# Three moves in the order of an attention and MLP kernel: a score tile, two squares and a quarter of a weight load

## The chip, the cores and the metric

The kernel runs on one core of a Trainium2 chip. The metric is the device time of one execution in microseconds; it is the median over several executions. The engines are named as in the profile: PE (matrix products), ACT (activation functions), DVE (vector work), POOL (vector work, and the software DMA queue q0), SP (issues DMAs on the hardware queue q1). Each engine does its instructions in the order of the program; only semaphores tie the engines together.

## The reference

Inputs are q, k, v of shape (8, 12, 448, 64), gains for the norms, and the weights of an MLP. The reference, cut to what matters:

```python
def rmsnorm(x, g):
    return x / sqrt(mean(x * x, -1) + 1e-06) * g
scores = matmul(rmsnorm(q, g_q), rmsnorm(k, g_k).T) / 8     # 448 x 448 for each of 96 heads
attn   = softmax(scores)
x      = matmul(attn, v)          # heads side by side: 3584 rows of 768
h      = x @ w_in                 # 768 x 2048
out    = (maximum(h, 0) + alpha * minimum(h, 0)) @ w_out    # 2048 x 768
```

## The kernel before

The work of attention is cut into 24 groups y of four heads, three groups (G = 3) for each of 8 batches. What happens to a group, with the function and the line that the profile shows:

- `load_qk` (L105): four DMAs on SP's queue bring q and k of the group as float32, each tile (`nat`) in two halves. Six `nat` tiles exist, so that three groups fit.
- `square` (L148, POOL from group 2 on), `reduce` (L154, DVE), `root` (L165 and L166, ACT: a logarithm and an exponential), `scale` (L171, POOL for most groups): the norm. Results are `sq`, `ss`, `rr`, `qs`.
- `turn_dma` (L181): from group 6 on (TD = 6) two DMA transposes on SP's queue turn `qs` into `qT` and `kT`; `turn` (L192, DVE) then multiplies `kT` by the gains. For earlier groups PE transposes (`tps`, L206) and DVE copies (L215, L217).
- `score` (L232, PE): one of seven tiles j of a group's scores, in PSUM (`sc`, two slots). `soft` (L246, ACT): its exponential, `expT`.
- `den` and `attv` (L261, PE): the sums and the products with v (`dn`, `av`, `avb`); `log` and `invert` (L278, L283, ACT); the normed result goes to `xT` (L310, L312, DVE).

The MLP is cut into units. `up(b, ft)` makes one of 16 tiles of h for batch b (six matmuls, L327, into `hT`, or `hTb`/`hTa` in other PSUM banks), then `ah` (L354, ACT) and `gT` (L355, DVE). `down(b0, t, oh)` makes 128 rows and one half oh of the outputs: 16 matmuls over the tiles of `gT` and `w_out_sb` (L365, `op` or `opa`), a copy (`osb`, L377) and DMAs of the output (L385).

A planner puts the score tiles into bursts n, and MLP units into the gap after each burst (`gaps[n]`). Its list `prep` holds calls that go ahead of a burst, its list `post` those that go behind the units of its gap. `at(n, ...)` and `after(n, ...)` fill these lists:

```python
def after(n, f, *a):
    post.setdefault(max(int(n), 0), []).append((f, a))
```

The bursts that matter here:

| burst | score tiles (group, tile) | other attention work | units in its gap |
|---|---|---|---|
| 10 (`lead`) | (3,0) (3,1) (3,2) | den and attv of group 2 | up 0 to 4 of batch 0 |
| 11 | (3,3) (3,4) | root and scale of group 5 | up 5, 6 |
| 12 | (3,5) (3,6) | PE transpose of group 4; v of batch 1 is loaded ahead of it | up 7, 8 |
| 13 | (4,0) (4,1) | reduce of group 6 | up 9, 10, 11 |
| 14 | (4,2) (4,3) | root and scale of group 6, its DMA transposes | up 12, 13 |
| 15 | (4,4) (4,5) | PE transpose of group 5 | up 14, 15 |
| 16, 17 | (4,6) (5,0) to (5,3) | den of groups 3 and 4; root of group 7 | down (0, t) for oh = 0, t = 0, 1 |
| 18 | (5,4) (5,5) (5,6) (6,0) | attv of groups 3 and 4 | down t = 2, oh = 0 |
| 19, 20 | group 6 | den, attv of group 5 | down t = 0 and t = 1, oh = 1 |
| 21 | (7,0) (7,1) | reduces of group 9 | up 0 to 3 of batch 1 |

Burst 10, in the text "group 2's burst", is special. Batch 0's attention is completed in it, so the MLP can begin. Units 0 to 3 are begun ahead of it with the products that don't need group 2 (`begin`, L342), and their remainder follows as units 0 to 3 of the gap. Units 2 and 3 share one PSUM tile, `hTb`. The third score tile (3,2) and its exponential are put between the units by the list `late`, whose entries hold the number of units after which a call is made.

w_in and w_out are loaded on POOL's queue, with a cast to float16. `load_w_out(c)` brings a quarter of w_out: c // 2 is the half oh of the outputs, c % 2 the half of the 16 weight tiles. `first` is 10, the burst of `lead`. The loads of v (`vt`, L114) use the same queue.

Of the kernel before, what the change touches and what calls it, by code (L numbers as in the profile page):

```python
# [21 lines left out]
def kernel(  # L22
# [19 lines left out]
    G = HH // 2  # L42
# [135 lines left out]
    def turn_dma(y):  # L178
        for nm in "qk":
            t = att.tile([128, J, 2, 64], FP16, name=f"{nm}T", tag=f"{nm}T", bufs=4)  # L180
            nc.sync.dma_start(  # L181
                out=t.rearrange("p j g c -> p j (g c)"),
                in_=qs[y, nm].rearrange("p j h d -> p (j h d)"),
                transpose=True,
            )
            qkT[y, nm] = t
# [38 lines left out]
    def score(y, j):  # L225
        qT, kT = qkT[y, "q"], qkT[y, "k"]
        sc = pss.tile([128, 2, 512], FP32, name="sc", tag="sc")
        m = 64 if y < EARLY else 32
        for c in range(64 // m):
            for par in range(2):  # L230
                for g in range(2):
                    nc.tensor.matmul(  # L232
                        out=sc[ds(64 * g + m * c, m), par, :S].rearrange(
                            "p (j c) -> p j c", j=J
                        ),
                        lhsT=kT[ds(64 * par, 64), j, g, ts(c, m)],
                        rhs=qT[ds(64 * par, 64), :, g, :],
                        start=True,
                        stop=True,
                    )  # L240
        scs[y, j] = sc

    def soft(y, j):
        if j == 0:
            expT[y] = att.tile([128, J, 2, S], FP16, name="expT", tag="expT", bufs=EB)
        nc.scalar.activation(  # L246
            out=expT[y][:, j], in_=scs[y, j][:, :, :S], func=AF.Exp,
            scale=QK_SCALE, bias=expb[:, 0:1],
        )
# [19 lines left out]
    def den(ys):  # L269
        dn = psa.tile([128, 2, 512], FP32, name="dn", tag="acc")  # L270
        over_keys(
            (dn[:, 0], dn[:, 1]), ys, lambda g, y, par, c, j: ones[ds(64 * g, 64), c]
        )
        rden[ys] = dn

    def log(ys):
        r = att.tile([128, 2, S], FP32, name="rden", tag="rden")
        nc.scalar.activation(out=r, in_=rden[ys][:, :, :S], func=AF.Ln)  # L278
        rden[ys] = r
# [55 lines left out]
    def begin(ft):  # L335

        if ft < 2:
            begun[ft] = bank("hT", False)
        elif ft == 2:
            t = psa.tile([128, 2, 512], FP32, name="hTb", tag="acc")  # L340
            begun[2], begun[3] = t[:, 0], t[:, 1]
        up_part(begun[ft], 0, ft, 0, G - 1)  # L342
# [66 lines left out]
    while m < NG * J or steps:  # L409
        n = len(bursts)  # L410
        while steps:
# [14 lines left out]
        late = both or n in dens and n in avs or any(  # L426
            y >= G for y in dens.get(n, avs.get(n, ()))
        )
        limit = 2 + late + (both and avs[n][0] >= G)
        bursts.append([])  # L430
        while len(bursts[n]) < limit and m < NG * J:
            y, j = divmod(m, J)
# [13 lines left out]
    def at(n, f, *a):  # L446
        prep.setdefault(max(int(n), 0), []).append((f, a))

    def after(n, f, *a):
        post.setdefault(max(int(n), 0), []).append((f, a))  # L450
# [9 lines left out]
    for y in range(G, NG):  # L460

        early = y < G + 2
        if early:
            n = turn_at[y - 1] + 1
        elif y == G + 2:
            n = den_at[G - 1]
        elif y == 2 * G:
            n = turn_at[y] - 4
        elif y % G == 1:
            n = den_at[y - 4] - 1  # L470
        elif y % G:
            n = den_at[y - G]
        else:
            n = av_at[y - 4]
        at(n - (6 if early else 4 if y <= 3 * G else 5), load_qk, y)
        for nm in "qk":
            after(n - 2, square, y, nm)
            if early:
                after(n, reduce, y, nm)
            else:  # L480
                jobs.setdefault(n, []).append((reduce, (y, nm)))
        roots[n + 1] = y
# [29 lines left out]
    first = av_at[G - 1]  # L512
# [92 lines left out]
    after(7, load_w_in, 2)  # L605
    after(8, load_w_in, 3)
    for c in range(4):
        after(first + c // 2 * 2, load_w_out, c)
    roots[3] = 2

    since = 2
    for n in range(NB):
        for f, a in prep.get(n, ()):
            f(*a)
        tiles = bursts[n]

        lead = n == den_at[G - 1]
        first_tiles = tiles[: 2 if lead else split.get(n, 2)]
        for t in first_tiles:
            score(*t)  # L620
            if n == den_at[G - 1] - 1 and t == tiles[-1]:
                begin(0)
                begin(1)
            elif lead and t == tiles[0]:
                soft(*t)
                den(dens[n])
                attv(avs[n], 0, True, (log, invert))
            elif lead and t == tiles[1]:
                begin(2)
        plain = lead or n not in dens and n not in avs  # L630
        wait = plain and not lead and gaps[n] and gaps[n][0][0] is up
        if lead:
            begin(3)
        for t in tiles[:1] if wait else tiles[1:2] if lead else first_tiles:
            soft(*t)
        if n in dens and not lead:
            den(dens[n])
        if n in avs and not lead:

            for half in (1, 0) if avs[n] == (0, 1) else (0,):  # L640
                attv(avs[n], half)
        for t in () if lead else tiles[len(first_tiles) : 3]:
            score(*t)
            soft(*t)
        if n in avs and len(avs[n]) == 2 and avs[n] != (0, 1):
            attv(avs[n], 1)
        for t in () if lead else tiles[max(len(first_tiles), 3) :]:
            score(*t)
            soft(*t)
        late = []  # L650
        if wait:
            late = [(1, soft, t) for t in tiles[1:]]
        if n in roots:
            y = roots[n]
            work = [(root, (y,)), (scale, (y, "q")), (scale, (y, "k"))]
            if lead:

                late = [(3, score, tiles[2]), (4, soft, tiles[2])]
            if lead or wait and y < TD:
                late += [(late[-1][0], f, a) for f, a in work]  # L660
            else:
                for f, a in work:
                    f(*a)
            if y >= TD:
                turn_dma(y)
        if n in dens and not lead:
            log(dens[n])
            if gaps[n] and gaps[n][0][0] is down:
                invert(dens[n])
            else:  # L670
                late = [(1, invert, (dens[n],))]
        done = 0

        spare_at, clock = [], 0.0
        taken = n + 1 in dens or n + 1 in avs or turns.get(n + 1, TD) < TD
        for k, (f, a) in enumerate(gaps[n]):
            free = 2.3 if n in dens else (0.1, 1.2, 0.0)[len(avs.get(n, ()))]
            since += 1
            if clock >= free and not turns.get(n, TD) < TD and (
                since > 2 and not (taken and k == len(gaps[n]) - 1) or free == 0.0 and k == 0  # L680
            ):
                spare_at.append(k)
                since = 0
            clock += DOWN if f is down else UP
        ups_first = gaps[n] and gaps[n][0][0] is up
        if ups_first and n in dens and not lead:
            for f, a in jobs.pop(n, ()):
                f(*a)
        turned = n in turns and gaps[n] and (turns[n] >= TD or turns[n] < 2 * G)
        if turned and not ups_first and turns[n] >= TD:  # L690
            jobs.setdefault(n, []).append((turn, (turns[n],)))
        elif turned:
            turn(turns[n])
        for k, (f, a) in enumerate(gaps[n]):
            spare = k in spare_at
            if f is down:
                down(*a, jobs.pop(n, ()), spare)
            else:
                f(*a, spare)
                done += 1  # L700
                if n in jobs and not (lead and done < 4):
                    g, c = jobs[n].pop(0)
                    g(*c)
                    if not jobs[n]:
                        del jobs[n]
                while late and done == late[0][0]:
                    _, g, c = late.pop(0)
                    g(*c)
        if not gaps[n] and n in turns:
            turn(turns[n])  # L710
        for _, g, c in late:
            g(*c)
        if n < den_at[G - 1] - 1 and plain and n not in turns:
            spin(1)
        for f, a in jobs.pop(n, []) + post.get(n, []):
            f(*a)
# [32 lines left out]
```

## Time and profile before

| what | value |
|---|---|
| median of 4 runs | 433.69 us (433.39 to 434.06) |
| the profiled execution's own time | 433.39 us |
| its span, first to last instruction | 431.5 us |
| granted clock of PE | 1.000 |
| busy PE, ACT, DVE, POOL | 416.3, 279.0, 203.3, 175.4 us |
| exponentials of scores (L246) | 168 of 1004 ns |
| squares on POOL (L148) | 44 of 1678 ns |
| scale on POOL (L171) | 44 of 1764 ns |
| reduce on DVE (L154) | 48 of 1078 ns |
| quarters of w_out (L133) | 4 of 768 KB, 11.9 us from issue to landing in the median |

The page gives for each group of instructions its busy time and the mean of one; a timeline's columns are start, duration, and in brackets the engine's idle time before it and what ended it. A wait that an engine other than PE has costs time only if PE waits for it in turn.

### The profile page before, as it was taken

What the parts mean: (1) busy time and instruction counts of PE and PEld (TensorE: products, weight loads), DVE (VectorE), ACT (ScalarE), POOL (GpSimd) and SP (SyncE); (2) the same over time, 40 slices, a digit from 0 to 9 for tenths busy, and PEclk for the clock granted to TensorE, in tenths of its full rate; (3) what the DMA queues carried; (4) which work ended last, traced back from release to release, by engine and by line L of the source; (5) the groups of instructions that cost most, each with busy time, mean ns of one, the idle gap of its engine ahead of it and who ended that gap; (6) DMA issues with size and microseconds to landing.
All of it is one profiled execution on the core that took longest, in us unless ns stands there. A gap on an engine that the chain in (4) does not pass through costs nothing.

```text
span 431.5 us, 11488 instructions
## 1 busy us (share of the span) xinstructions
PE 416.3 (96%) x4964; PEld 216.2 (50%) x4964; DVE 203.3 (47%) x304; ACT 279.0 (65%) x385; POOL 175.4 (41%) x133
## 2 busy tenths in 40 slices
PE   7789899899999999999999999999999999999996
PEld 3344344444455445544555445554555445555564
DVE  3755764455545463545444463545453353233421
ACT  4998878678976677767667577757757577132300
POOL 5799695493184407380283506371163000000000
PEclk9999999999999999999999999999999999999999
DMA  8999999999579724877059843774073300211133
GB/s 186 235 235 217 157 212 181 215 188 206 126 111 197 179 76 72 164 147 181 20 100 192 180 111 64 150 152 113 20 126 79 77 1 21 56 38 33 23 73 75
DMA packets 70387, 53.85 MB, mean 125 GB/s; under 512 B 37424, under 2 KB 70336, under 8 KB 70336
## 3 DMA queue, kind: packets, MB, share of 16 engines
q1 hardware_dynamic: 55536, 40.19, 43.2%
q0 software_dynamic: 13984, 11.81, 18.5%
q10 hardware_dynamic: 816, 1.11, 1.1%
q8 instruction: 39, 0.64, 0.6%
q14 instruction: 12, 0.10, 0.1%
HBM read 45.62 MB, written 11.01 MB: 131 GB/s over the span
## 4 chain that ended last, share of the span: by engine, by line
PE 78%; DMA 3%; DVE 3%; ACT 1%; POOL 0%; issue 0%
PE op L365 27%; PE hT L327 19%; PE hTa L327 10%; PE opa L365 6%; PE sc L232 6%; PE dn L261 4%; PE av L261 4%; DMA kT<-qs 3%; PE avb L261 2%; DVE ss L154 1%; ACT expT L246 1%; DVE osb L377 1%; DVE gT L355 1%; DVE xT L312 1%; POOL sq L148 0%
## 5 line engine op out<-in xcount | busy, mean ns | idle before, releaser
L246 ACT ACTIVATE expT<-sc,expb 128x896 f16<-128x896 f32 x168 | 161.5, 1004 | 36.2 <-PE sc L232 35.3
L171 POOL TENSOR_TENSOR qs<-nat,rr 128x896 f16<-128x896 f32 x44 | 76.8, 1764 | 149.1 <-issue 79.2
L365 PE MATMUL op<-w_out_sb,gT 128*128 128x384 f16 (+1 forms) x752 | 126.3, 323 | 0.0
L365 PEld LDWEIGHTS <-gT 128*128 128x128 f16 x912 | 85.8, 98 | 65.4 <-issue 12.8
L327 PEld LDWEIGHTS <-w_in_sb 128*128 128x128 f16 x768 | 73.2, 98 | 74.2 <-issue 9.7
L327 PE MATMUL hT<-xT,w_in_sb 128*128 128x448 f16 x510 | 107.2, 353 | 1.4 <-DVE gT L355 1.1
L354 ACT ACTIVATE ah<-hT,cols 128x448 f16<-128x448 f32 x85 | 53.8, 634 | 44.1 <-PE hT L327 44.0
L355 DVE TENSOR_TENSOR gT<-hT,ah 128x448 f16<-128x448 f32 x85 | 52.8, 624 | 51.4 <-ACT ah L354 51.3
L148 POOL TENSOR_TENSOR sq<-nat 128x896 f32<-128x896 f32 x44 | 72.9, 1678 | 8.2 <-DMA nat<-in_q_dram 6.3
L377 DVE COPY osb<-op 128x384 f32<-128x384 f32 (+1 forms) x47 | 25.8, 548 | 86.0 <-PE op L365 86.0
L232 PE MATMUL sc<-qT,kT 64*32 64x448 f16 (+1 forms) x1092 | 53.6, 356 | 5.9 <-ACT expT L246 3.9
L154 DVE TENSOR_REDUCE ss<-sq 128x14 f32<-128x896 f32 x48 | 50.7, 1078 | 9.4 <-ACT sq L146 5.9
L327 PE MATMUL hTa<-xT,w_in_sb 128*128 128x448 f16 x246 | 53.2, 352 | 0.0
L354 ACT ACTIVATE ah<-hTa,cols 128x448 f16<-128x448 f32 x41 | 26.0, 634 | 31.3 <-PE hTa L327 31.3
L355 DVE TENSOR_TENSOR gT<-hTa,ah 128x448 f16<-128x448 f32 x41 | 25.6, 623 | 26.0 <-ACT ah L354 26.0
L232 PEld LDWEIGHTS <-kT 64*32 64x32 f16 (+1 forms) x1092 | 15.2, 93 | 38.4 <-issue 32.5
L365 PE MATMUL opa<-w_out_sb,gT 128*128 128x384 f16 x160 | 27.7, 326 | 0.6 <-DVE xT L312 0.6
L312 DVE TENSOR_TENSOR xT<-av,rden 128x896 f16<-128x896 f32 x16 | 17.5, 1091 | 17.5 <-PE av L261 14.1
L261 PEld LDWEIGHTS <-vt 64*32 64x32 f16 (+1 forms) x1260 | 18.9, 94 | 13.2 <-issue 2.2
L261 PE MATMUL dn<-expT,ones 64*32 64x448 f16 (+1 forms) x812 | 24.2, 350 | 0.9
L261 PE MATMUL av<-expT,vt 64*32 64x448 f16 (+1 forms) x812 | 24.1, 349 | 0.0
L278 ACT ACTIVATE rden<-dn 128x896 f32<-128x896 f32 x16 | 14.5, 907 | 7.3 <-PE dn L261 7.3
(45 smaller groups left out, 159.1 us busy)
## 6 DMA issues: line engine op xcount, KB each, us to landing
out_dram<-osb SPq DMA_DIRECT2D x109, 96.0 KB, 2.3
nat<-in_q_dram SPq DMA_DIRECT2D x46, 224.0 KB, 5.2
nat<-in_k_dram SPq DMA_DIRECT2D x46, 224.0 KB, 6.6
vt<-in_v_dram POOLq DMA_DIRECT2D x16, 336.0 KB, 7.1
w_in_sb<-in_moe_w_in_dram POOLq DMA_DIRECT2D x12, 256.0 KB, 7.4
w_out_sb<-in_moe_w_out_dram POOLq DMA_DIRECT2D x4, 768.0 KB, 11.9
nat<-in_q_dram ACTq DMA_DIRECT2D x2, 224.0 KB, 4.6
nat<-in_k_dram ACTq DMA_DIRECT2D x2, 224.0 KB, 5.8
```

The lines of the kernel that those rows point to most:

```text
L148: nc.gpsimd.tensor_mul(out=sqf, in0=src, in1=src)
L154: nc.vector.tensor_reduce(out=ss_t[y][:, "qk".index(nm)].rearrange("p h j -> p (h j)").unsqueeze(2), in_=sqs[y, nm], axis=AXIS_X, op=ALU.add,)
L171: eng.tensor_mul(out=t.rearrange("p j h d -> p h j d"), in0=nat[y, nm], in1=rr_t[y][:, "qk".index(nm)].unsqueeze(3).broadcast_to((128, 2, ...
L232: nc.tensor.matmul(out=sc[ds(64 * g + m * c, m), par, :S].rearrange("p (j c) -> p j c", j=J), lhsT=kT[ds(64 * par, 64), j, g, ts(c, m)], r ...
L246: nc.scalar.activation(out=expT[y][:, j], in_=scs[y, j][:, :, :S], func=AF.Exp, scale=QK_SCALE, bias=expb[:, 0:1],)
L261: nc.tensor.matmul(out=accs[g][ds(m * h, m), :S], lhsT=weights(g, y, par, ts(c, m), j), rhs=expT[y][ds(64 * g, 64), j, par, :], start=(j = ...
L312: nc.vector.tensor_mul(out=x, in0=av[:, :, :S], in1=r)
L327: nc.tensor.matmul(out=hT[:, :S], lhsT=w_in_sb[:, g * G + i, ts(ft, 128)], rhs=xT[b][:, g, i, :], start=(i == 0 and g == 0), stop=(i == G ...
L354: nc.scalar.activation(out=ah, in_=hT[:, :S], func=AF.Copy, scale=alpha_sb[:, ft : ft + 1])
L355: nc.vector.tensor_max(out=gT[:, ft, ds((b & 1) * S, S)], in0=hT[:, :S], in1=ah)
L365: nc.tensor.matmul(out=ops[c][:, :PW], lhsT=gT[:, ft, ts(t, 128)], rhs=w_out_sb[:, ft, ds(oh * OH + c * PW, PW)], start=(ft == 0), stop=(f ...
L377: nc.vector.tensor_copy(out=o[:, ts(c, PW)], in_=ops[c][:, :PW])
```

## The change

Three calls move. The third score tile of burst 10 and its exponential go behind the second unit of the gap rather than behind the third and the fourth; root and scale of group 4, which follow them in the list, stay behind the fourth. The squares of group 6 go behind burst 10 rather than 11. The fourth quarter of w_out goes behind burst 14 rather than 12; the first three stay.

```diff
         for nm in "qk":
-            after(n - 2, square, y, nm)
+            if y != 2 * G:
+                after(n - 2, square, y, nm)
             if early:
...
     for c in range(4):
-        after(first + c // 2 * 2, load_w_out, c)
+        after(first + (0, 0, 2, 4)[c], load_w_out, c)
+    for nm in "qk":
+        after(first, square, 2 * G, nm)
     roots[3] = 2
...
             if lead:
 
-                late = [(3, score, tiles[2]), (4, soft, tiles[2])]
+                late = [(2, score, tiles[2]), (2, soft, tiles[2])]
             if lead or wait and y < TD:
-                late += [(late[-1][0], f, a) for f, a in work]
+                late += [(4 if lead else 1, f, a) for f, a in work]
```

In the order that results, POOL's work behind scale of group 4 reads: before, two quarters of w_out, scale of 5, squares of 6, two loads of v, two quarters of w_out, scale of 6, squares of 7, scale of 7; changed, two quarters, squares of 6, scale of 5, two loads of v, one quarter, scale of 6, squares of 7, one quarter, scale of 7. On PE four matmuls move ahead of those that complete units 2 and 3, on ACT one exponential moves ahead of the two ah of these units. The orders of DVE and of SP are the same as before.

## The prediction

> **What bounds the kernel now.** I read the page first, then the waits of PE and of DVE between 42 and 98 us, then the timelines of ACT, DVE and PE in that stretch, and last the DMA view in narrow windows.
>
> ```profile
> span 431.5 us, 11488 instructions
> PE 416.3 (96%) x4964; PEld 216.2 (50%) x4964; DVE 203.3 (47%) x304; ACT 279.0 (65%) x385; POOL 175.4 (41%) x133
> ```
>
> PE is the bound. It is idle for some 15 us in all; the larger part of its waits lies before 37 us, where the change touches nothing. From 98 us on it is dense. So only its idle time between 42 and 98 us can be won:
>
> ```profile
> PE sc L232 <- ACT expT L246: 1.4, 3, 1.1
> PE hT L327 <- DVE gT L355: 1.1, 2, 1.0
> PE opa L365 <- DVE xT L312: 0.6, 1, 0.6
> PE sc L232 <- DVE kT L192: 0.6, 1, 0.6
> ```
>
> The columns are the total wait, its count and the longest. These four rows, 3.7 us, are all the prize there is. The timelines give their causes: 46.57 us (1.08, the third score tile's exponential), 60.51 us (0.96, the reduces of tile group 6), 78.37 and 79.36 us (0.56 and 0.61, the transposed keys of group 6).
>
> ```profile
> 43.66 0.63 ACT L354 ACTIVATE ah<-hTb,cols 128x448 f16<-128x448 f32 x1
> 44.99 0.64 ACT L354 ACTIVATE ah<-hTb,cols 128x448 f16<-128x448 f32 x1 [0.69 <-DVE gT L355]
> 45.52 1.00 ACT L246 ACTIVATE expT<-sc,expb 128x896 f16<-128x896 f32 x1
> 46.41 0.32 ACT L165 ACTIVATE rr<-ss,epsb 128x28 f32<-128x28 f32 x1
> ```
>
> ACT is full from 45 to 52 us. A PE stall here is covered by a queue of ACT work, and moving one ACT instruction doesn't shorten the queue.
>
> ```profile
> 77.86 0.45 DVE L192 TENSOR_SCALAR kT<-kT,gain 128x896 f16<-128x896 f16 x1 [3.17 <-DMA kT<-qs]
> 78.23 1.08 DVE L312 TENSOR_TENSOR xT<-av,rden 128x896 f16<-128x896 f32 x1
> ...
> 90.50 0.45 DVE L192 TENSOR_SCALAR kT<-kT,gain 128x896 f16<-128x896 f16 x1 [2.72 <-DMA kT<-qs]
> 90.87 1.08 DVE L312 TENSOR_TENSOR xT<-av,rden 128x896 f16<-128x896 f32 x1
> ```
>
> DVE, which works in order, stands twice for a DMA transpose: for group 6 until 77.8 us and for group 7 until 90.5 us. Behind each stands an xT that PE needs. This is the second bound: from 53 to 90 us the DMA engines have no idle stretch longer than about a microsecond.
>
> ```profile
> q0 software_dynamic: 521, 0.39, 88.2%
> q1 hardware_dynamic: 525, 0.13, 35.9%
> ```
>
> That is 68 to 70.8 us: POOL's queue q0 (w_out) and SP's q1 (the transposes) move packet for packet, 187 per us each. The transposes' pieces are small, so they crawl.
>
> **Step A, the third score tile.** Nothing is added: four matmuls and one exponential (0.89 us from start to start) move ahead of units 2 and 3. PE then does score (3,2) at 42.8 and unit 4 at 43.9 as before. Its slot is free at 44.6 instead of 46.5, so score (3,4) no longer waits: 1.08 saved at that place. But ACT's order is now ah0 42.53, ah1 43.06, exponential 43.59, ah2 44.48; gT2 follows at 45.15 (0.67 after its ah, as before), ah3 waits for it as in the row above, 45.81; Ln and Exp of group 4, and ah4 at 46.82 against 46.89. The same ACT work ends at the same time. On DVE gT3 is late (46.48 for 45.66), then the reduce of group 5 (1.0 us) at 47.02 for 46.20, and gT4 at 48.02 for 47.54. Unit 6 needs gT4's PSUM bank: 48.69 for 48.22, so PE stalls there. The next two score tiles get back 0.2, since one of them had waited for ACT at 49.83. Sum: PE is **0.25 later** at unit 7 (51.24 for 50.99). The 1.08 turns into a wait for a bank.
>
> **Step B, the squares of group 6.** POOL does two squares (3.31 us for both) before rather than after scale of group 5 (3.35). The reduces then start when DVE is free: 0.34 + 0.02 of waiting goes, and with the gT that precedes them the bank of unit 11 is free at 60.19 instead of 60.45, A's 0.25 included. So B is worth 0.53, and PE is **0.28 early** at 60.2. Price: scale of group 5 ends at 58.7 instead of 55.5; its reader, the PE transpose at 62.3, covers that with 3.6 us; beyond those each microsecond would be PE's. v's loads leave at the same time.
>
> **Step C, the last quarter of w_out.** POOL's 0.9 us of issue moves behind scale of group 6 and the squares of group 7. From 47.0 POOL runs without a gap: 3.3 scale, 1.8 two quarters, 3.3 squares, 3.3 scale, 1.4 v, 0.9 third quarter, so scale of group 6 starts at 61.0 instead of 61.9 and SP's transposes are issued 0.9 earlier (SP's order is unchanged; the nat loads behind them move up too). The last quarter goes at about 67.6 instead of 61.0, and nothing on POOL waits for it (scale of group 7 waits for ACT until 72.9).
>
> What this does to the transposes depends on q0. The third quarter landed at 72.3; with pairing from 66.5 on q0 runs dry at about 70.5. The trace's nearest row for the start: the first quarter was issued at 50.4 and the window 50.3 to 52.7 shows no packet of q0, full rate comes about a microsecond later. So the last quarter joins between 69.9 and 71.2: just as q0 would run dry. The Trainium skill (DMA: Bandwidth & Descriptors, Specifications) gives a software DMA a first byte after about 1 us: 68.6, well before, no gap, all 1,792 transpose packets paired, 1792 / 187 = 9.6 us plus the 0.75 us stop that the trace has at 71: keys of group 6 at 77.8 as before, and C worth nothing. By the trace's 2.3 us and slow start I allow a gap of 0.1 us. In a gap the transposes go at 640 packets per us or more (86 to 88 us: 1,249 small ones in 2 us, a stop included), so a microsecond of gap brings them 2.5 to 3.5 us forward. I take 0.1 to 0.15 us, hence 0.4.
>
> **What passes on.** PE's 0.28 reaches 77.5 us, where it waits again for the keys of group 6: what counts from there is the DMA. The keys of group 7 stand on q1 behind eight nat loads, so everything ahead must be moved first. The same page (Issuing engines are not separate DMA queues) says that all queues end on the same 16 engines and interleave. That speaks against the change: an order on a queue makes no bandwidth, and the keys of group 7 would still land at 90.5; PE could then gain the 0.35 us between the end of xT (91.95) and unit 0 (92.34), and lose it by 97.73, where the chain xT, reduces, gT holds it. The trace says that the mix matters a little: q0 with transposes 0.52 MB in 2.8 us (192 GB/s in its window), nat alone 214 GB/s (78 to 85), q0 with nat 224 (53.5 to 57.5). What is taken from the first mix and put beside nat saves a few tenths. So I carry 0.4 at 90.5, 0.4 at 97.7 and, PE being dense then, 0.4 at the end. Of A's and B's 0.28 nothing is added: it is spent waiting.
>
> Sum: profiled execution 433.39 (span 431.5 and 1.9 around it) less 0.4 is 433.0; the median of the runs lies 0.3 above the profiled one, so 433.69 - 0.4 = **433.3**.
>
> **Rivals.** *q0 runs dry for a while* (faster). If the last quarter joins 0.3 us or more after the third has drained, the transposes finish a microsecond or more earlier, the last quarter goes beside nat, and both waits of DVE shrink. PE then keeps 0.28 + 0.56 + 0.61 = 1.45, with the 0.16 at 97.73 at most 1.6. For it: the slow start of q0 at 52.7 us. Against: by my times the queue still holds something. It would give about 432.4.
>
> *The last quarter is late for PE* (slower). The first down unit of the right half of the outputs starts at 84.4 and reaches the ninth weight tile, which the last quarter brings, at 85.7. In the trace the w_out loads took 8.7 to 16.3 us to land; from 67.6 that is 76 to 83.9. If nat, now beside it, holds it to 19.5 us, it lands at 87.1 and PE stands 1.4 us, of which the 0.35 of slack at 92.3 is won back: about 434.7. It decides from a landing after 85.7. Against: it has 18 us, longer than any w_out load took.
>
> *The moves only exchange waits* is the main case with its gain at zero; it lies within 0.2%.
>
> **How the numbers follow.** 0.2%, 0.87 us, is about what a measurement of this kernel can tell from no change. Main case 0.50: 432.8 to 433.9, nearly all within that bound, 0.41, and 0.09 beyond it, since a gap is worth three times its length. q0 dry 0.32: 431.9 to 432.8, of which 0.31 faster. Late quarter 0.18: 0.16 slower, 0.02 within. So faster 0.40, same 0.44, slower 0.16. The main case's own range is 432.8 to 433.9; with the other two, 432.0 to 434.7.
>
> **What would show it.** A: no wait at 46.57, but one of some 0.4 us before unit 6, on gT. B: no wait of the reduces near 57 us, PE's wait of 0.96 down to about 0.7. C: kT's DMA still 11 to 13 us long and DVE's two waits for it about where they are. The prediction is wrong if q0 shows a stretch without packets near 71 us and the keys of group 6 land before 76.5; if PE waits inside op near 85 us; or if PE at 97.7 has moved by more than 0.9.

## The result, and the profile after

The changed kernel takes 432.81 us in the median (431.04 to 437.81, 43 runs), the kernel before, run beside it, 433.96 us (432.94 to 436.57, 64 runs). The ratio is 0.9973, 95% interval 0.9961 to 0.9986: faster by 1.2 us where the forecast was 0.4. That is beyond the 0.2% that was to count as no change. Both rivals of the prediction, the "faster" and the "slower" one, can be seen in the one profiled execution below.

In part of the executions of most kernels, before's too, PE's granted clock is 0.992 to 0.997 and the time some 2 to 4 us longer, so the table of experiments also gives the median of the runs at 0.998 or more ("full clock").

The page after, its first rows:

```profile
span 431.8 us, 11487 instructions
PE 416.3 (96%) x4964; PEld 216.0 (50%) x4964; DVE 204.4 (47%) x304; ACT 279.0 (65%) x385; POOL 175.3 (41%) x133
```

PE's busy time is the same to the tenth, so the gain is idle time. DVE is 1.1 us busier, though it has the same 304 instructions; that is explained below. The execution that was profiled (433.53 us) is one of the slower ones of this kernel, and its timeline is 0.30 us behind that of before ahead of any change (the four matmuls that complete units 0 and 1 start at 42.25 for 41.95). Where I compare times of PE below, I take these 0.30 off. PE's waits from 42 to 98 us (total, count, longest):

```profile
PE hT L327 <- DVE gT L355: 2.2, 2, 1.7
PE op L365 <- DMA w_out_sb<-in_moe_w_out_dram: 1.7, 1, 1.7
PE sc L232 <- ACT expT L246: 0.3, 2, 0.2
```

Of the four rows of before, the keys of group 6 (`sc` behind L192) and the normed result (`opa` behind `xT`) are gone, 0.6 us each. That for the exponential is gone but for two waits of 0.3 in all. In their place stand a longer wait for `gT` and a new one, for w_out, which before had none. This is where the two of `gT` stand, on PE's timeline:

```profile
48.97 1.30 PE L327 MATMUL hT<-xT,w_in_sb 128*128 128x448 f16 x6 [1.74 <-DVE gT L355]
...
60.46 1.30 PE L327 MATMUL hT<-xT,w_in_sb 128*128 128x448 f16 x6 [0.42 <-DVE gT L355]
```

The first is unit 6, the place of step A; the second, which was 0.96 us in the kernel before, is at that of step B. On DVE's timeline the keys of group 6 and of group 7 come at 75.06 and 90.02, for 77.86 and 90.50 before:

```profile
75.06 1.53 DVE L192 TENSOR_SCALAR kT<-kT,gain 128x896 f16<-128x896 f16 x1 [0.42 <-DMA kT<-qs]
76.51 1.08 DVE L312 TENSOR_TENSOR xT<-av,rden 128x896 f16<-128x896 f32 x1
...
90.02 0.45 DVE L192 TENSOR_SCALAR kT<-kT,gain 128x896 f16<-128x896 f16 x1 [1.76 <-DMA kT<-qs]
```

DVE's wait of 3.17 for group 6 is down to 0.42. But L192 then takes 1.53 us instead of 0.45: the extra busy time. The reason for the early keys is in the DMA view from 71 to 74.5 us. Before:

```profile
q0 software_dynamic: 516, 0.40, 86.8%
q1 hardware_dynamic: 517, 0.12, 38.8%
```

After, the same stretch (packets, MB, share of the 16 engines):

```profile
q1 hardware_dynamic: 916, 0.37, 88.5%
q0 software_dynamic: 33, 0.02, 6.6%
```

Before, the weights and the transposes take turns, one for one. After, q0 is all but empty for 3.5 us, and q1 has finished the transposes and is at its nat loads (0.37 MB for 0.12). The gap in q0 on which step C turned is there, and it is long. What it costs is in the chain of work that ended last (start, duration):

```profile
64.59 3.21 POOL sq L148 x2
67.81 18.36 DMA w_out_sb<-in_moe_w_out_dram
86.16 0.04 issue
86.20 1.46 PE op L365 x8
```

The last quarter, issued at 67.81, takes 18.36 us to land. PE has begun `op` at 83.07 and stops after eight tiles until 86.20, 1.66 us.

### The profile page after: what moved, and what is told of

Same layout as the page of the kernel before. It is cut to its first block, busy times and chain, and to the rows that moved or that the text cites. A ratio compares the mean times of both kernels' runs of the same rounds, so it can differ in the third digit from the quotient of the medians.

```text
span 431.8 us, 11487 instructions
## 1 busy us (share of the span) xinstructions
PE 416.3 (96%) x4964; PEld 216.0 (50%) x4964; DVE 204.4 (47%) x304; ACT 279.0 (65%) x385; POOL 175.3 (41%) x133
## 4 chain that ended last, share of the span: by engine, by line
PE 83%; DMA 6%; ACT 5%; DVE 4%; POOL 1%; issue 1%; SPq 0%; ACTq 0%
PE op L365 27%; PE hT L327 21%; PE hTa L327 11%; PE sc L232 7%; PE opa L365 6%; PE av L261 4%; PE dn L261 4%; DMA w_out_sb<-in_moe_w_out_dram 4%; ACT expT L246 3%; PE avb L261 2%; DMA nat<-in_k_dram 1%; DVE ss L154 1%; PE tps L206 1%; DVE gT L355 1%; POOL sq L148 1%; DVE osb L377 1%
## 5 line engine op out<-in xcount | busy, mean ns | idle before, releaser
L365 PE MATMUL op<-w_out_sb,gT 128*128 128x384 f16 (+1 forms) x752 | 126.5, 323 | 1.7 <-DMA w_out_sb<-in_moe_w_out_dram 1.7
L365 PEld LDWEIGHTS <-gT 128*128 128x128 f16 x912 | 85.7, 98 | 66.6 <-issue 14.1
L365 PE MATMUL opa<-w_out_sb,gT 128*128 128x384 f16 x160 | 27.7, 326 | 0.0
L312 DVE TENSOR_TENSOR xT<-av,rden 128x896 f16<-128x896 f32 x16 | 17.4, 1090 | 17.5 <-PE av L261 14.2
```

Of the source, the lines that this page charges most:

```text
L312: nc.vector.tensor_mul(out=x, in0=av[:, :, :S], in1=r)
L365: nc.tensor.matmul(out=ops[c][:, :PW], lhsT=gT[:, ft, ts(t, 128)], rhs=w_out_sb[:, ft, ds(oh * OH + c * PW, PW)], start=(ft == 0), stop=(f ...
```

## The experiments

Each kernel ran beside the kernel before on the same chip. "C" is the late last quarter, "B" the early squares, "A" the score tile.

| kernel | median, runs | ratio (95%) | median at full clock (before: 433.91 to 433.99) |
|---|---|---|---|
| A alone | 433.86, 14 | 0.9986 (0.9971 to 1.0) | 433.86 |
| B alone | 434.58, 22 | 1.0004 (0.9991 to 1.0018) | 433.85 |
| C alone | 433.01, 21 | 0.9977 (0.9964 to 0.999) | 433.01 |
| B and C | 433.73, 14 | 0.9992 (0.9971 to 1.0013) | 433.42 |
| full change again | 433.54, 14 | 0.9983 (0.9964 to 1.0002) | 433.52 |
| full, no read of the last quarter in that unit | 435.6, 22 | 1.0013 (0.999 to 1.0035) | 432.87 |
| full, last quarter ahead of squares 7 | 433.56, 22 | 0.9988 (0.9975 to 1.0) | 433.49 |
| full, last quarter in two loads | 434.51, 22 | 1.0009 (0.9994 to 1.0025) | 434.19 |
| full, gain of group 7 on ACT | 432.83, 22 | 0.9969 (0.995 to 0.9988) | 432.83 |
| both of: no late read, gain on ACT | 432.0, 7 | 0.9931 (0.9905 to 0.9957) | 432.0 |
| full, group 9 two bursts later | 432.33, 16 | 0.9957 (0.9938 to 0.9976) | 432.29 |
| the same without A | 433.24, 21 | 0.9974 (0.9956 to 0.9993) | 432.91 |

**A alone.** The calls for the squares and for w_out are put back.

```diff
-            if y != 2 * G:
-                after(n - 2, square, y, nm)
+            after(n - 2, square, y, nm)
...
-        after(first + (0, 0, 2, 4)[c], load_w_out, c)
-    for nm in "qk":
-        after(first, square, 2 * G, nm)
+        after(first + c // 2 * 2, load_w_out, c)
```

> Only the score tile moves (step A). Theory (the DMA decides): the wait of 1.08 us at the score tile goes, a wait for gT's PSUM bank of 1.5 to 1.8 us stands before unit 6 instead, PE is about 0.25 us late at unit 7, and this is swallowed by the wait for group 6's keys, which land where they did (77.8 us +- 0.4); time within 0.3 us of before. Rival (PE's own stalls of the MLP's start decide): the time falls by 0.5 to 1.0 us.

Its waits of PE from 42 us on:

```profile
PE hT L327 <- DVE gT L355: 2.6, 3, 1.7
PE sc L232 <- DVE kT L192: 0.7, 1, 0.7
PE opa L365 <- DVE xT L312: 0.6, 1, 0.6
```

The wait for the exponential is exchanged for one of 1.74 for `gT` at 48.22, and both waits for the keys of group 6 stay (transposes 12.69 us, landed 77.44). The interval ends at 1.0: no gain clear of the noise, and no loss.

**B alone.** w_out and the list `late` are put back.

```diff
-        after(first + (0, 0, 2, 4)[c], load_w_out, c)
+        after(first + c // 2 * 2, load_w_out, c)
...
-                late = [(2, score, tiles[2]), (2, soft, tiles[2])]
+                late = [(3, score, tiles[2]), (4, soft, tiles[2])]
-                late += [(4 if lead else 1, f, a) for f, a in work]
+                late += [(late[-1][0], f, a) for f, a in work]
```

> Only the squares of group 6 move (step B). Theory (the DMA decides): PE's wait of 0.96 us near 60.5 us falls to some 0.4, PE reaches the down units about 0.5 us early and waits there that much longer for group 6's keys, whose transposes still take 11 to 12.5 us; time 0 to 0.3 us below before. Rival (PE's stalls of the MLP's start decide): 0.5 us below before.

```profile
PE sc L232 <- DVE kT L192: 1.5, 1, 1.5
PE sc L232 <- ACT expT L246: 1.4, 3, 1.1
...
PE hT L327 <- DVE gT L355: 0.4, 1, 0.4
```

PE's waits again: that for `gT` falls from 0.96 to 0.42, and that for the keys of group 6 grows to 1.5 (transposes 12.97 us). The time that B wins at 60 us is spent waiting at 79. In the table's last column it is where before is (433.85).

**C alone.** The squares and `late` are put back; only w_out's last quarter moves.

```diff
-            if y != 2 * G:
-                after(n - 2, square, y, nm)
+            after(n - 2, square, y, nm)
...
-    for nm in "qk":
-        after(first, square, 2 * G, nm)
...
-                late = [(2, score, tiles[2]), (2, soft, tiles[2])]
+                late = [(3, score, tiles[2]), (4, soft, tiles[2])]
```

> Only the last quarter of w_out moves (step C). Theory (queue q0 runs dry for some 3 to 4 us, the transposes go unpaired): keys of group 6 land near 75 to 76 us instead of 77.8, both PE waits of 0.56 and 0.61 us are gone, the last quarter takes 17 to 19 us and PE waits inside the down unit near 85 us for 0 to 1.7 us, by the execution; time 0.2 to 1.2 us below before. Rival (the gain is A's and B's, C only brings the late load): at before or up to 1 us above it.

```profile
PE sc L232 <- ACT expT L246: 1.4, 3, 1.1
PE hT L327 <- DVE gT L355: 0.9, 1, 0.9
PE op L365 <- DMA w_out_sb<-in_moe_w_out_dram: 0.6, 1, 0.6
```

The two waits of before outside C's reach are unchanged; the two for the keys of group 6 are gone, and the wait for w_out is there (landing 17.6 us after its issue). The transposes took 10.42 us and landed at 74.82. Its ratio, 0.9977, is that of the whole change within both intervals, and of the three parts C is the only one that is faster by itself beyond its interval.

**B and C.** Only `late` is put back.

```diff
-                late = [(2, score, tiles[2]), (2, soft, tiles[2])]
+                late = [(3, score, tiles[2]), (4, soft, tiles[2])]
-                late += [(4 if lead else 1, f, a) for f, a in work]
+                late += [(late[-1][0], f, a) for f, a in work]
```

> The squares and the last quarter move, the score tile stays (B and C). Theory: as the full change without A's 0.25 us, but PE then comes 0.25 us sooner to the late quarter and waits for it that much longer, so 0 to 0.3 us below the full change, 1.0 to 1.5 us below before. Rival (the score tile's move carries the gain): about before, at most 0.5 us below.

The last quarter landed 18.5 us after its issue and PE stood 2.08 us in `op`. The interval takes in 1.0 as well as the ratio of C alone, so on the time it settles nothing: 1.0 to 1.5 us were expected, and 0.9992 lies where its rival (the gain is A's) had put it. C alone, and the last row of the table, are faster without A, which speaks against that rival. The trace shows the exchange again, at a worse price.

**The full change again**, the same source as after, measured together with the three that follow.

> The full change once more, beside the three others on the same chip: 0.5 to 1.7 us below before; keys of group 6 near 75 us; PE's wait for the last quarter near 86 us between 0.5 and 2.1 us, another value than in the first profile, if the theory is right that this landing differs from execution to execution.

Transposes 12.05 us, landed 76.81; 1.25 us in `op` (landing 18.1 us). The same kernel has less than half of the gain here: 433.52 at full clock for 432.74 in the 40 such runs of after. Its interval takes in 1.0. The executions of this kernel differ: here the transposes are nearly as slow as before (12.5 us), and q0 is less empty (163 packets from 71 to 74.5 us, for 33 in after). The middle half of its 14 runs spans 432.5 to 434.4, of after's 43 runs 431.9 to 433.8.

**Without the late read.** Every unit but one is as in the change; the first unit of the right half reads the third quarter twice.

```diff
-                    rhs=w_out_sb[:, ft, ds(oh * OH + c * PW, PW)],
+                    rhs=w_out_sb[:, ft % 8 if (b0, t, oh) == (0, 0, 1) else ft, ds(oh * OH + c * PW, PW)],
```

> The full change, but the first down unit of the right half (t = 0, oh = 1) reads the third quarter of w_out twice instead of the third and the last one, so nothing waits for the last quarter there; that unit's output is another. Theory (the full change wins by an emptied queue and gives part of it back at the late quarter): PE's wait of 1.7 us near 86 us is gone, units of batch 1 begin right behind xT (about 91.5 us), where 0.2 to 0.4 us are lost again; time 0.4 to 1.3 us below the full change, 1.6 to 2.4 below before. Rival (the wait hides another one right behind it, group 7's keys): no more than 0.2 us below the full change.

The wait in `op` was gone, and the kernel was not faster for it in the ratio, whose interval takes in 1.0. At full clock it is 0.65 us below the full change measured beside it (432.87 for 433.52), where 0.4 to 1.3 was expected, but its middle half there, 431.7 to 435.0, takes in all of that of the other: the time settles nothing. The profiled execution (437.09 us, one of the slowest of the 22) has a new wait of PE, 3.97 us at 94.09, for L192 of group 7. DVE, then POOL:

```profile
89.22 4.82 DVE L192 TENSOR_SCALAR kT<-kT,gain 128x896 f16<-128x896 f16 x1 [2.80 <-DMA kT<-qs]
93.95 1.08 DVE L312 TENSOR_TENSOR xT<-av,rden 128x896 f16<-128x896 f32 x1
```

```profile
89.06 1.37 POOL L114 DMA_DIRECT2D vt<-in_v_dram  x2
90.43 3.34 POOL L171 TENSOR_TENSOR qs<-nat,rr 128x896 f16<-128x896 f32 x2
```

An instruction of 0.45 us took 4.82, and ended 0.27 us after POOL's run of v loads and scale (93.77). In after, L192 at 75.06 ended 0.25 us after the scale that it met (76.34):

```profile
73.01 3.33 POOL L171 TENSOR_TENSOR qs<-nat,rr 128x896 f16<-128x896 f32 x2 [4.25 <-issue]
```

The Trainium skill (SBUF — State Buffer, "Who interferes with whom") says that DVE, in the modes in which it uses two ports, and GpSimd share a pair of ports that one instruction holds to its end, while the other engine is blocked fully. These two rows agree with it, as L192 ends when POOL ends; that L192 uses two ports no run here shows.

**Last quarter ahead of the squares of group 7.** Everything else as in the change; POOL issues it 3.3 us sooner.

```diff
-    for c in range(4):
-        after(first + (0, 0, 2, 4)[c], load_w_out, c)
+    for c in range(3):
+        after(first + (0, 0, 2)[c], load_w_out, c)
...
+        if n == first + 4:
+            load_w_out(3)
```

> The full change, but POOL issues the last quarter between scale of group 6 and the squares of group 7, 3.3 us sooner (64.6 instead of 67.8). Theory (what counts is whether q0 runs dry before the last quarter joins): it joins at 67 to 69 us, ahead of the draining at 70 to 71, there is no or little gap, the keys of group 6 land at 77 to 78 as before, no wait for the last quarter near 86; time 0 to 0.4 us below before. Rival (what counts is that the 0.9 us of issue leaves the way of scale of group 6): keys at 75 to 76 and no late quarter, time 1.2 to 2.2 us below before.

The DMA view from 71 to 74.5 us, and two of PE's waits:

```profile
q0 software_dynamic: 567, 0.43, 78.7%
q1 hardware_dynamic: 562, 0.14, 31.0%
```

```profile
PE sc L232 <- DVE kT L192: 1.4, 1, 1.4
PE opa L365 <- DVE xT L312: 0.6, 1, 0.6
```

With the queue never dry, the pairing is back, the transposes take 13.96 us (landed 78.21), both waits for the keys are back, and none for w_out. So without the gap in q0 the moved issue brings no early keys (the kT transpose is issued as early here, at 64.25 for 64.62 in after). On the time this kernel and the full change measured beside it can't be told apart (433.49 and 433.52 at full clock), so what the gap is worth is read from the waits in the traces, not from these medians. And a gap alone isn't always enough, as is seen two runs further on. The runs lie close together now: the middle half spans 433.4 to 433.8, 0.4 us for after's 1.9.

**Last quarter in two loads of 384 KB**, the first at the old place, the second at the new one.

```diff
+        if part is not None:
+            n //= 2
+            lo += part * n
...
+    after(first + 2, load_w_out, 3, 0)
+    after(first + 4, load_w_out, 3, 1)
```

> The full change, but the last quarter of w_out goes in two loads of 384 KB: the first at its old place behind the third quarter, the second at its new place behind the squares of group 7. Theory: q0 runs dry later (73 to 74 us), the transposes still sprint at the end, keys of group 6 land near 75.5 to 76.5, and the second half, short, lands before 84 us, so PE waits for neither; time 1.3 to 2.2 us below before, 0.3 to 1.0 below the full change. Rival (a later draining leaves no gap worth having): keys at 77 to 78, time within 0.5 us of before.

My theory for it fell: the first half filled the gap wholly (511 packets of q0 from 71 to 74.5), the transposes took 13.78 us, and PE stood 1.93 and 0.61 us for the keys. It is slower than after, the intervals (0.9994 to 1.0025, 0.9961 to 0.9986) don't meet; that of the full change measured beside it (0.9964 to 1.0002) it does meet. It is a second case, beside the one above, of no gap and late keys.

**Gain of group 7 on ACT**, so that DVE has no L192 near 90 us.

```diff
+            if y == 7:
+                return
...
+            if y == 8:
+                t = qkT[7, "k"].rearrange("p j g c -> p (j g c)")
+                nc.scalar.activation(out=t, in_=t, func=AF.Copy, scale=gain[:, 0:1])
```

> The full change, but the gain of group 7's keys is multiplied by ACT (behind group 8's root) instead of DVE. Theory (a fast DVE instruction from SBUF to SBUF, L192, can't start while POOL runs, and this makes the slow executions): no L192 over 1.8 us is left, xT no longer stands behind group 7's keys; the spread of the full-clock runs narrows from 431-435.5 to 431-433.5, the median 0.3 to 0.8 us below the full change, with PE's wait for the last quarter (0.5 to 2 us) left. Rival (the spread is all from the last quarter): as the full change.

The time is after's. The runs at full clock still reach from 430.95 to 436.43, so L192 near 90 us is not all that spreads them; their middle half is narrower (432.1 to 433.4, for 431.8 to 433.5 in after and 432.5 to 434.3 in the full change again), so whether it is a part of the spread stays open. The profiled execution (436.19) is one of the slowest, and a bad case:

```profile
PE op L367 <- DMA w_out_sb<-in_moe_w_out_dram: 2.8, 1, 2.8
...
PE sc L234 <- DVE kT L194: 1.1, 1, 1.1
```

Here the last quarter took 21.3 us, and the keys of group 6 were late as well (78.02, transposes 13.7 us). The wait of 1.1 is theirs; the lines of this kernel stand two lower (L194 for L192, L367 for L365). Yet the gap in q0 was there, from 71 to 74.5 us:

```profile
q1 hardware_dynamic: 830, 0.21, 112.1%
q0 software_dynamic: 44, 0.03, 7.6%
```

So a gap alone doesn't bring the keys early: q1 moved nearly as many packets as in after (830 for 916), but it hadn't come to the nat loads (0.21 MB for 0.37). Why is open; the edit itself acts only near 90 us.

**Both: no late read, gain on ACT.** The two edits together:

```diff
-                    rhs=w_out_sb[:, ft, ds(oh * OH + c * PW, PW)],
+                    rhs=w_out_sb[:, ft % 8 if (b0, t, oh) == (0, 0, 1) else ft, ds(oh * OH + c * PW, PW)],
...
+            if y == 7:
+                return
...
+                nc.scalar.activation(out=t, in_=t, func=AF.Copy, scale=gain[:, 0:1])
```

> As e5 (one down unit reads the third quarter twice, its output is another), and the gain of group 7's keys on ACT. Theory (in e5 the wait of 4.0 us for L192 took what the late quarter had cost): neither wait is left, score (7,0) starts near 90.2 us, time 2.0 to 3.0 us below before with a narrow spread. Rival (e5 was slow for another reason): still about before.

The long wait for L192 is gone; PE waits 0.3 us for ACT's version. But in the profiled execution (434.3, the slowest of the seven) the keys of group 6 are late in spite of a gap, as in the run before (49 packets of q0 from 71 to 74.5, transposes 13.8 us), and PE waits 1.2 and 0.6 us for them. 432.0 us and a ratio of 0.9931 are the best here, over 7 runs, but the unit reads other weights. Beside the row "gain on ACT" it puts the cost of the late quarter at 0.8 us, with intervals that overlap (0.995 to 0.9988 and 0.9905 to 0.9957).

**Group 9 two bursts later.** Loads, squares, reduces, root and scale of group 9, all of which fall near 75 to 97 us, go two bursts later, so that the last quarter has fewer nat loads beside it.

```diff
-            n = av_at[y - 4]
+            n = av_at[y - 4] + (2 if y == 3 * G else 0)
```

> The full change, with the loads, squares, reduces, root and scale of group 9 two bursts later. Theory (the last quarter is late because eight nat loads share the DMA engines with it; group 9 has slack until 118 us): q0 runs at more than 105 packets per us when only four nat loads and the transposes of group 7 are beside it, the last quarter lands near 83 to 84.5 us, the keys of group 7 at 84 to 87; PE's waits at 78, 79, 86 and behind xT are gone or under 0.5 us; time 2.0 to 3.0 us below before, 1 to 2 below the full change. Rival (nothing is gained by emptying the queue before 90 us, since the waits come back with the next loads): within 0.5 us of the full change.

```profile
PE hT L327 <- DVE gT L355: 2.7, 3, 1.7
PE op L365 <- DMA w_out_sb<-in_moe_w_out_dram: 0.4, 1, 0.4
PE sc L232 <- ACT expT L246: 0.3, 2, 0.2
```

The waits from 42 to 103 us: the late quarter costs 0.43 (landing 17.1 us), the keys of group 6 land at 74.96, those of group 7 at 85.55 rather than 89.99 (1.0 us of this is the timeline of the execution: units 0 and 1 are completed from 41.22 on, for 42.25 in after), and the reduces of group 9, now at 101 us, bring one wait of 0.52. The rate of q0 beside nat was not above the 105 per us expected: 99 to 116 from 74 to 80 us. The middle half of the runs spans 432.1 to 432.6. At 0.9957 (0.9938 to 0.9976) it is faster than before, and its median is the lowest of the kernels that compute the whole; its interval meets that of the change itself, measured at another time.

**The same without A.** Group 9 as above, and `late` put back:

```diff
-            n = av_at[y - 4]
+            n = av_at[y - 4] + (2 if y == 3 * G else 0)
...
-                late = [(2, score, tiles[2]), (2, soft, tiles[2])]
+                late = [(3, score, tiles[2]), (4, soft, tiles[2])]
```

> As e11, with the score tile at its old place (no step A). Theory: where no DMA wait swallows it, A's 0.25 us becomes visible, so this is 0.1 to 0.4 us below e11. Rival (A gains): 0.3 us or more above e11.

0.9974 against 0.9957, with intervals that overlap. That A costs something was not seen. Whether it helps stays open: the kernel with A is the faster one in all three comparisons (A alone 0.9986; the full change 0.9973 for 0.9992 of B and C; here), each time within the noise.

## Why the prediction was right or wrong

**The time is inside the range, the mechanism was another.** The median, 432.81, lies in the stated range (432.0 to 434.7) and just inside the lower edge of the main case (432.8 to 433.9). That is luck: the main case forecast a gain of 0.4 from transposes that stay paired with q0, and two of the three signs that the prediction itself named as showing it wrong came true. q0 was all but empty near 71 us with the keys of group 6 at 75.04, before 76.5, and PE waited inside `op` near 85 us. The third did not: PE at 97.7 had moved by 0.24. A gain and a price that the main case both put at nearly nothing cancel in part.

**Step A was right on the timeline.** It said that the 1.08 would turn into a wait for a bank, and that unit 6 would start at 48.69 and unit 7 0.25 later. Less the 0.30, unit 6 starts at 48.67 and unit 7 0.20 later. The "wait of some 0.4 us" under what would show it was mis-stated: 0.4 is the delay of unit 6, while the wait itself is 1.74, since PE now arrives there a microsecond and more sooner. ACT's order shows why nothing is won:

```profile
43.88 1.01 ACT L246 ACTIVATE expT<-sc,expb 128x896 f16<-128x896 f32 x1
44.77 0.64 ACT L354 ACTIVATE ah<-hTb,cols 128x448 f16<-128x448 f32 x1
46.10 0.63 ACT L354 ACTIVATE ah<-hTb,cols 128x448 f16<-128x448 f32 x1 [0.69 <-DVE gT L355]
```

The exponential goes first, and the `ah` that PE's banks hang on come 0.8 us later, as worked out. What A is worth in time stays open, as said above.

**Step B was right.** PE 0.28 early at 60.2 was forecast; it is 0.35. B alone spends it at the keys of group 6, as "nothing is added: it is spent waiting" says.

**Step C is where the prediction failed, in the gap: its length, and what it is worth.** The issue time was right (67.6, measured 67.81). "So the last quarter joins between 69.9 and 71.2" was not, nor "I allow a gap of 0.1 us". Between 71 and 74.5 q0 moved 33 packets, and counted by the microsecond it reached 100 and more only from 75 on, 7 us after the issue. The gap was some 4 us, as against 0.1 to 0.15. The estimate rested on one row, the first quarter's start (2.3 us without a packet, full rate a microsecond later). C alone shows the later start cleanly: issued at 67.57, with no packet of q0 from 71.75 to 73.0 and then 1,040 up to 88 us (0.79 MB, the whole quarter). So its first packet came more than 5.4 us after the issue. In after 1,040 packets are left at 73.0 as well, 5.2 us after the issue; by this count the few before that are the end of the third quarter. The first byte after about a microsecond that the prediction took from the Trainium skill (DMA: Bandwidth & Descriptors, Specifications) is further off still.

The rule for what a gap is worth, 2.5 to 3.5 us for each microsecond, did not hold either. A gap of 4 us brought the keys of group 6 2.8 us forward (75.04 for 77.83), 3.1 less the 0.30. The rate of 640 packets per us wasn't reached: q1, which beside q0 had moved 187, moved 473 from 70 to 71 us, then 56 (a stop that before has at that place too) and 352 from 72 to 73. With all profiled executions set on one clock by the start of units 0 and 1, L192 of group 6 starts 1.5 to 3.1 us sooner than before in seven of the nine with the late quarter, and 0.2 and 0.3 us later in the two with the gain on ACT. In after both waits of PE went, as the first rival has it.

**The rivals were not alternatives.** With the keys early, PE keeps 0.35 + 0.56 + 0.61 = 1.5 at 83 us (1.64 by the starts of `op`: 83.07 less 0.30 for 84.41); rival 1 had put 1.45. The measured median gain of 1.2 would be this with part of it lost again; that isn't shown. And the last quarter, beside nat, landed at 86.16, not far from rival 2's 87.1; "it has 18 us, longer than any w_out load took" didn't protect it, since it took 18.4. What I didn't see is that the first rival moves the point from which the second decides: PE reaches the ninth tile 1.5 us sooner, 84.5 on the timeline of after, so the same landing costs more. One gap makes both. They should have been one case, with a gain of 1.5 less a wait of nought to 2.8 (the profiled executions here show 0.38, 0.43, 0.62, 1.25, 1.66, 2.08 and 2.79). In the profiled execution the two cancel: PE at 97.97 for 97.73 is 0.06 early, less the 0.30. The median is better than that one execution; if it is this wait that sets the executions apart, in most the landing comes sooner. No trace of such an execution of after was taken; C alone and group 9 later, with waits of 0.6 and 0.4, are the nearest.

**The keys of group 7** were to land at 90.5, as the order on a queue makes no bandwidth: 89.99, so nearly. 0.4 was carried on from there; 0.5 is what the row shows, 0.8 less the 0.30.

**Not in the prediction: POOL holding up DVE.** L192 took 1.53 us at 75.06, and the times point to POOL. In after it costs PE nothing, since the `xT` behind it has time. PE paid for it in one profiled execution, that without the late read.

## What to carry to other kernels

Two transfers that take turns packet for packet can be parted by letting the queue of the large one run dry: here the small packets then went at 352 and 473 per us for 187, a stop apart. It is not sure to help: in two profiled executions of nine the gap was there and the small transfer landed as late as before. And the large one starts again late (over 5 us after its issue here), so find its reader and the time that the reader will have once the first wait is gone. When an edit has a gain and a price from the same cause, forecast them as one case, and look at the spread of the runs too: a median that hangs on where a transfer lands differs between two sets of runs of the same kernel.

## What was not expected of the hardware

- A software queue that had drained took more than 5.4 us from issue to its first packet beside DMA transposes (C alone; 5.2 or more in after) and about 7 us until it moved 100 packets per us; at the first quarter it was 2.3 and 3.3. Why is open; no run took the transposes or POOL's work away from it.
- The same load, issued between 67.2 and 68.0 us with the same nat loads beside it, landed after 17.4 to 18.5 us in the profiled executions of five kernels, and after 20.5 and 21.3 us in two, both with the gain of group 7 on ACT. The edit acts only near 90 us; whether it or chance is behind this, one execution of each doesn't tell.
- L192, 0.45 us alone, took 1.53, 1.77 (C alone) and 4.82 us beside POOL, and ended each time 0.25 to 0.27 us after an instruction of POOL; three shorter cases near 75 us (0.59, 0.71 and 0.72) ended 0.25 to 0.26 us after the scale that they met. In the longest case it was not let in between two instructions of POOL. But an L192 that began 0.16 us into the loads of v (the full change again) or 0.56 us into them (B and C) took 0.45, while the longest one began 0.16 us into them too, so what decides this is open. That POOL is the cause rests on the times and on the page; the runs show only that without L192 on DVE the long wait is gone.
